# Attention two sequences ahead, 1/sqrt spread through DRAM, one rotation of four PSUM pairs

## The chip, the cores and the metric

The kernel runs on one core of a Trainium2 chip. Its engines are PE (TensorE, matrix products), DVE (VectorE), ACT (ScalarE), POOL (GpSimd) and SP (SyncE, which here issues nearly all DMAs); each runs its own list of instructions in order and waits for others on semaphores. SBUF and PSUM are the on-chip memories of 128 partitions, DRAM the memory outside. The metric is the time of one execution on the device in microseconds. S + x stands for x us after PE begins a sequence.

## The reference

Eight sequences ("batch") of 576 positions go through three stages: linear attention with a norm over each head's 64 features, a gated product with a causal convolution, and a mixing stage.

```python
# attention: q, k, v are (8, 8 heads, 576, 64)
kv = np.einsum('bhsd,bhse->bhde', k, v)
out = np.einsum('bhsd,bhde->bhse', q, kv)
rms = np.sqrt(np.mean(out * out, axis=-1, keepdims=True) + 1e-06)
x = (out / rms * g_norm)            # heads side by side: (8, 576, 512)
# gated product
for k in range(5):
    gate_pre += conv_w[k][None, None, :] * xp[:, k:k + S, :]   # xp: 4 zero rows ahead
gate = 1.0 / (1.0 + np.exp(-gate_pre))
x = gate * (x @ w_val) @ w_out
# mixing
theta = x @ w_theta
yr = np.einsum('ts,bsd->btd', w_tok_r, x * np.cos(theta))
yi = np.einsum('ts,bsd->btd', w_tok_i, x * np.sin(theta))
u = x + yr + yi
out = u + np.maximum(u @ w_ch, 0.0)
```

## The kernel before, in words

Feature d of x lies on a partition, with positions along the free axis, so a 512 x 576 activation is four tiles of 128 x 576. A large product runs in three passes, high x high, high x low, low x high (`product`, L259 to L266); `parts` (L65) makes the high part on ACT (L68) and the low part, the rest, on DVE (L69). Attention and the small selecting products are plain float32, and each of their instructions leaves two records in the trace.

The first phase is the loop over eight sequences at L385. For sequence b these steps exist:
- `key_value` (L171): k transposed times v, 64 x 64 for each head, in PSUM tile kvp, copied by ACT to kvs (L187). It may do all four head pairs, or two of them ("units" of pairs; the table UNITS says how many in which sequence, LEAD how many sequences are done whole at the start).
- `attention` (L189): o = q times kvs in four groups, each two feature tiles by half of the positions (L202); ACT squares each into sq (L206) and copies it, scaled by g_norm, to x (L207). Then `sums` (L214) adds the squares of each head by products with an indicator, into ss: 32 rows for each of the four feature tiles, of which eight are used (two heads by NB = 4 blocks of TB = 144 positions). Twelve DVE operations (L221 to L227) make y, the inverse square root.
- `normalize` (L230): products with the selecting matrix sel (L243) spread y's rows over the 64 partitions of each head into PSUM yb; DVE multiplies x by it in place (L246), and `parts` makes xh and xl. There is one xh and one xl.
- `conv` (L251): the five taps, one on ACT (L253), four on DVE (L255, in acc), then a sigmoid on ACT (L256).
- `value` (L268): four results v of 24 products each (two PSUM banks, 576 positions); DVE multiplies each by the gate in acc (L278), and `parts` makes gh and gl.
- `first` (L284): four results y of 24 products each with w_out. y0 and y1 first use 18 of theirs, and the last six follow when the fourth gh and gl are there. ACT copies y to yo, and SP writes it to DRAM (ydram, L295).

In sequence i the loop does value(i) with the four groups of attention(i + 1) between its results, key/value products of later sequences, then first(i) with the four spreads and multiplies of normalize(i + 1) between its parts. Sequence 0 is prepared ahead of the loop, with key_value(1). Decoding of later weights (w_th and w_tok) goes in at low priority in sequences 1 to 6.

PSUM holds three pairs of banks (pool pd, for v, o, yb and y) and two single banks (pool pk, for kvp and ss). Inputs come by SP in program order: q (`load_q`, buffers q), k and v (`load_kv`, four buffers kv). START is the order of the first loads. No table orders the instructions; a scheduler puts them on each engine when the kernel is built, by priorities and its own costs, and each engine then runs its list as it stands.

The second phase, from L448, computes theta, cosine and sine, token and channel products from what the first left in DRAM.

## Time and profile before

| | us |
|---|---|
| three runs | 779.54, 775.77, 779.06 (median 779.06) |
| the profiled execution | 778.61 |
| its span | 776.7 |
| PE busy in it | 734.6 (95%) |
| DVE busy in it | 532.1 (69%) |
| ACT busy in it | 338.3 (44%) |
| start of theta, the second phase | 342.06 |
| DMA, mean over the span | 126 GB/s |

The page shows the busy time of each engine and groups of instructions by line. A group's row gives the output and inputs by name, the shape, the count, busy time and mean ns of one, and then the idle time of the engine just ahead of them with what ended it. A row of a timeline gives start, length, engine, line, and in brackets the idle time before it and its releaser. A row of windows gives each engine's busy time in a stretch of the span, the granted clock of PE as a share, the DMA engines' share and GB/s. Windows here begin where PE starts a sequence's value product; sequence 0's is at 41.93.

### The profile page before, as it was taken

What the parts mean: (1) busy time and instruction counts of PE and PEld (TensorE: products, weight loads), DVE (VectorE), ACT (ScalarE), POOL (GpSimd) and SP (SyncE); (2) the same over time, 40 slices, a digit from 0 to 9 for tenths busy, and PEclk for the clock granted to TensorE, in tenths of its full rate; (3) what the DMA queues carried; (4) which work ended last, traced back from release to release, by engine and by line L of the source; (5) the groups of instructions that cost most, each with busy time, mean ns of one, the idle gap of its engine ahead of it and who ended that gap; (6) DMA issues with size and microseconds to landing.
All of it is one profiled execution on the core that took longest, in us unless ns stands there. A gap on an engine that the chain in (4) does not pass through costs nothing.

```text
span 776.7 us, 14376 instructions
## 1 busy us (share of the span) xinstructions
PE 734.6 (95%) x5872; PEld 680.0 (88%) x5872; DVE 532.1 (69%) x942; ACT 338.3 (44%) x562; POOL 18.3 (2%) x64
## 2 busy tenths in 40 slices
PE   1588999999999999899999999999999999999998
PEld 1376888888888889898999999899899999999998
DVE  4289778989989796958796493663863853845604
ACT  2246545465636463548462261441651612713301
POOL 3000000000000000000000000000000000000000
PEclk9889999999999999999999999999999999999999
DMA  9956862757373211943606315045033071151101
GB/s 249 261 144 185 261 186 86 192 202 230 131 239 104 62 47 47 271 157 107 185 24 170 101 54 145 35 132 153 2 122 109 31 187 55 45 149 38 62 1 62
DMA packets 72929, 97.56 MB, mean 126 GB/s; under 512 B 10656, under 2 KB 41504, under 8 KB 72864
## 3 DMA queue, kind: packets, MB, share of 16 engines
q1 hardware_dynamic: 72288, 94.55, 40.8%
q0 software_dynamic: 576, 2.10, 0.8%
q8 instruction: 46, 0.75, 0.4%
q14 instruction: 19, 0.16, 0.1%
HBM read 65.66 MB, written 30.97 MB: 124 GB/s over the span
## 4 chain that ended last, share of the span: by engine, by line
PE 77%; DVE 14%; DMA 4%; ACT 3%; issue 2%; SPq 0%; ACTq 0%; DVEq 0%
PE u L508 10%; PE u L506 10%; PE u L507 10%; DVE acc L255 4%; PE c L266 4%; PE c L265 4%; PE c L264 4%; PE y L264 3%; PE th L454 3%; PE th L452 3%; PE th L453 3%; DMA kv<-in_kvm_dram 3%; PE y L266 3%; PE y L265 3%; PE v L264 3%; PE v L265 2%
## 5 line engine op out<-in xcount | busy, mean ns | idle before, releaser
L511 DVE TENSOR_TENSOR f<-u,f 128x288 f32<-128x288 f32 x64 | 26.5, 454 | 128.1 <-PE u L508 128.0
L255 DVE SCALAR_TENSOR_TENSOR acc<-x,cw,acc 128x576 f32<-128x576 f32 x128 | 97.7, 812 | 0.0
L68 ACT ACTIVATE uh<-f 128x288 fp32r<-128x288 f32 x64 | 26.2, 444 | 151.1 <-DVE f L511 151.1
L264 PE MATMUL y<-gh,woh 128*128 128x288 f32 x256 | 79.9, 312 | 3.6 <-DVE acc L278 2.9
L264 PE MATMUL v<-xh,wvh 128*128 128x288 f32 x256 | 79.0, 309 | 3.3 <-ACT wvh L68 3.0
L265 PE MATMUL y<-gh,wol 128*128 128x288 f32 x256 | 77.0, 301 | 0.0
L266 PE MATMUL y<-gl,woh 128*128 128x288 f32 x256 | 76.8, 301 | 0.0
L265 PE MATMUL v<-xh,wvl 128*128 128x288 f32 x256 | 76.1, 298 | 0.3 <-DVE wvl L69 0.3
L266 PE MATMUL v<-xl,wvh 128*128 128x288 f32 x256 | 75.8, 297 | 0.0
L264 PE MATMUL c<-uh,wch 128*128 128x288 f32 x256 | 75.4, 295 | 0.0
L266 PE MATMUL c<-ul,wch 128*128 128x288 f32 x256 | 75.4, 295 | 0.0
L265 PE MATMUL c<-uh,wcl 128*128 128x288 f32 x256 | 75.4, 294 | 0.0
L264 PEld LDWEIGHTS v<-xh,wvh 128*128 128x128 f32 x256 | 48.8, 191 | 14.5 <-issue 8.3
L264 PEld LDWEIGHTS y<-gh,woh 128*128 128x128 f32 x256 | 49.3, 193 | 7.6 <-DVE acc L278 3.4
L454 PE MATMUL th<-wth,yl 128*128 128x512 f32 x128 | 50.3, 393 | 0.0
L453 PE MATMUL th<-wtl,yh 128*128 128x512 f32 x128 | 50.0, 391 | 0.0
L452 PE MATMUL th<-wth,yh 128*128 128x512 f32 x128 | 50.0, 391 | 0.0
L265 PEld LDWEIGHTS y<-gh,wol 128*128 128x128 f32 x256 | 49.5, 194 | 0.5 <-DVE wol L69 0.2
L266 PEld LDWEIGHTS y<-gl,woh 128*128 128x128 f32 x256 | 49.1, 192 | 0.6
L265 PEld LDWEIGHTS v<-xh,wvl 128*128 128x128 f32 x256 | 49.0, 191 | 0.5 <-DVE wvl L69 0.5
L266 PEld LDWEIGHTS v<-xl,wvh 128*128 128x128 f32 x256 | 48.6, 190 | 0.1
L265 PEld LDWEIGHTS c<-uh,wcl 128*128 128x128 f32 x256 | 48.0, 188 | 0.3
(187 smaller groups left out, 1979.9 us busy)
## 6 DMA issues: line engine op xcount, KB each, us to landing
kv<-in_kvm_dram SPq DMA_DIRECT2D x32, 512.0 KB, 6.2
q<-in_qt_dram SPq DMA_DIRECT2D x32, 288.0 KB, 4.5
yd<-yo SPq DMA_DIRECT2D x32, 288.0 KB, 2.2
f<-yd SPq DMA_DIRECT2D x32, 288.0 KB, 3.6
out_dram<-f SPq DMA_DIRECT2D x64, 144.0 KB, 1.8
sd<-fT SPq DMA_DIRECT2D x64, 128.0 KB, 2.5
yt<-sd SPq DMA_DIRECT2D x8, 1024.0 KB, 5.4
raw_tk<-in_w_tok_dram SPq DMA_DIRECT2D x10, 512.0 KB, 5.3
```

The costliest lines, as they stand in the source:

```text
L68: one = nc.scalar.activation(h, src, AF.Copy)
L255: nc.vector.scalar_tensor_tensor(a, x[:, m, k:k + S], cw[:, m * 5 + k:m * 5 + k + 1], a, ALU.mult, ALU.add)
L264: nc.tensor.matmul(ps, wh[:, m, ks], xh[:, k, tsl], start=(k == 0), stop=False)
L265: nc.tensor.matmul(ps, wl[:, m, ks], xh[:, k, tsl], start=False, stop=False)
L266: nc.tensor.matmul(ps, wh[:, m, ks], xl[:, k, tsl], start=False, stop=(k == 3))
L452: nc.tensor.matmul(ps, yh[:, k, :], wth[0][:, k, :], start=(k == 0), stop=False)
L453: nc.tensor.matmul(ps, yh[:, k, :], wth[1][:, k, :], start=False, stop=False)
L454: nc.tensor.matmul(ps, yl[:, k, :], wth[0][:, k, :], start=False, stop=(k == 3))
L506: nc.tensor.matmul(ps[:, :HS], zh[:, ms], wkh[:, j, sl], start=(i == 0), stop=False)
L507: nc.tensor.matmul(ps[:, :HS], zh[:, ms], wkl[:, j, sl], start=False, stop=False)
L508: nc.tensor.matmul(ps[:, :HS], zl[:, ms], wkh[:, j, sl], start=False, stop=(i == 8))
L511: nc.vector.tensor_tensor(f[:, m, sl], ps[:, :HS], f[:, m, sl], ALU.add)
```

## The change

- TB goes from 144 to 72, so y has 64 used rows of 72 instead of 32 of 144: eight blocks of sums, each half as wide.
- key_value does a whole sequence at a time, between the first and the second value result of the sequence two before it; UNITS, LEAD and NBD go.
- attention(i + 2) runs in sequence i: one half (both groups) ahead of the fourth value result, the other half after it; its sums and y follow in first(i), after the second part's last products.
- From sequence 2 on (SPREAD), y is written to DRAM (rdram, new L228) and read back spread over the partitions by two DMAs of 64 partitions (new L233) into yb in SBUF, of which there is one; DVE multiplies from there, two operations of 1152 elements (new L246). Sequences 0 and 1 keep the products with sel (new L254, L257).
- normalize(i + 1) stands between value(i) and first(i).
- One pool of four PSUM pairs serves all; kvp and ss take a pair each and use one bank of it.
- kvs has two buffers instead of four, q two instead of three. START brings k and v of sequence 1 and its q earlier, and three chunks of w_out later. attention(1) and its sums stand ahead of the loop.

```diff
-TB = 144
+TB = 72
 NB = S // TB
...
-NBD = 4
-
-START = "v0 k0 k1 v1 k2 k3 v2 q0 q1 q2 q3 c0 v3 o0 o1 k4 k5 k6 k7 o2 q4 q5 o3 q6 q7"
+
+START = "v0 k0 k1 v1 k2 k3 v2 q0 q1 q2 q3 c0 v3 o0 k4 k5 k6 k7 o1 q4 q5 q6 q7 o2 o3"
 WVFIRST = 3
-WOFIRST = 2
-LEAD = 3
-UNITS = (0, 2, 4, 2, 4, 4, 0, 0, 0)
+SPREAD = 2
...
+    def one_bank(name):
+        return pd.tile([P, 2, 512], F32, tag="pd", name=name)[:, 0, :]
...
+    rdram = [dr.tile([P, TB], F32, tag=f"rd{b}", name=f"rd{b}") for b in range(B)]
...
-    pd = pd_stack.enter_context(tc.tile_pool(name="pd", bufs=3, space=PS))
-    pk = pd_stack.enter_context(tc.tile_pool(name="pk", bufs=2, space=PS))
+    pd = pd_stack.enter_context(tc.tile_pool(name="pd", bufs=4, space=PS))
...
-                q.append(px.tile([P, 2, S], F32, tag="q", bufs=3, name=f"q{b}_{g}"))
+                q.append(px.tile([P, 2, S], F32, tag="q", bufs=2, name=f"q{b}_{g}"))
...
-    def key_value(b, kv, p0=0):
-
-        ps = pk.tile([P, 512], F32, tag="pk", name=f"kvp{b}_{p0}")
-        n = len(kv) // 2
-        for g in range(n):
+    def key_value(b, kv):
+
+        ps = one_bank(f"kvp{b}")
+        for g in range(2):
...
-        if b not in kvs_of:
-            kvs_of[b] = pa.tile([P, NP, D], F32, tag="kvs", bufs=NBD, name=f"kvs{b}")
-        nc.scalar.activation(kvs_of[b][:, p0:p0 + 2 * n, :], ps[:, 0:2 * n * D].rearrange("p (a e) -> p a e", e=D), AF.Copy)
+        kvs_of[b] = pa.tile([P, NP, D], F32, tag="kvs", bufs=2, name=f"kvs{b}")
+        nc.scalar.activation(kvs_of[b], ps[:, 0:NP * D].rearrange("p (a e) -> p a e", e=D), AF.Copy)
...
-                yield x
-
-        sums = pk.tile([P, 512], F32, tag="pk", name=f"ss{b}")[:, :TB]
+            yield x
+
+        sums = one_bank(f"ss{b}")[:, :TB]
...
+        if b >= SPREAD:
+
+            nc.sync.dma_start(out=rdram[b], in_=y)
+            yb = px.tile([P, NM, S], F32, tag="yb", bufs=1, name=f"yb{b}")
+            src = rdram[b].rearrange("(k r) x -> k (r x)", k=NM)
+            for i in range(2):
+                rows = src[:, i * S:(i + 1) * S].unsqueeze(0).to_broadcast([D, NM, S])
+                nc.sync.dma_start(out=yb[i * D:(i + 1) * D], in_=rows)
+            y = yb
         yield x, y
...
-            for g in range(2):
-                yb = two_banks(f"yb{b}_{h}_{g}")
-                for t in range(HS // TB):
-                    for j in range(2):
-                        k = 2 * g + j
-                        rows = slice(32 * k, 32 * (k + 1))
-                        nc.tensor.matmul(yb[:, j, t * TB:(t + 1) * TB], sel[rows, h * HS // TB + t, :], y[rows, :],
-                                         start=True, stop=True, tile_position=(32 * k, 0))
-                ch = slice(2 * g, 2 * g + 2)
-                last = nc.vector.tensor_tensor(v[:, ch], yb, v[:, ch], ALU.mult)
-                if g == 1:
-                    parts(xh[:, :, sl], xl[:, :, sl], v)
-                yield (x, xh, xl), last
+            if b >= SPREAD:
+                last = nc.vector.tensor_tensor(v, v, y[:, :, sl], ALU.mult)
+            else:
+                for g in range(2):
+                    yb = two_banks(f"yb{b}_{h}_{g}")
+                    for t in range(HS // TB):
+                        for j in range(2):
+                            k = 2 * g + j
+                            rows = slice(32 * k, 32 * (k + 1))
+                            nc.tensor.matmul(yb[:, j, t * TB:(t + 1) * TB], sel[rows, h * HS // TB + t, :], y[rows, :],
+                                             start=True, stop=True, tile_position=(32 * k, 0))
+                    ch = slice(2 * g, 2 * g + 2)
+                    last = nc.vector.tensor_tensor(v[:, ch], yb, v[:, ch], ALU.mult)
+            parts(xh[:, :, sl], xl[:, :, sl], v)
+            yield (x, xh, xl), last
...
-            between()
+            between(m)
...
-            last, _ = parts(gh[:, m, :], gl[:, m, :], g)
+            parts(gh[:, m, :], gl[:, m, :], g)
...
         part(0, range(3))
         part(1, range(3))
-        between()
         part(0, (3,))
-        between()
         part(1, (3,))
         between()
         part(2, range(4))
-        between()
         part(3, range(4))
...
     *_, xy = attention(0, qs.pop(0))
+    *_, (xs, last) = normalize(0, *xy)
     key_value(1, kvs.pop(1))
-    *_, (xs, last) = normalize(0, *xy)
+    *_, xy = attention(1, qs.pop(1))
     sg = [conv(0, m, xs[0]) for m in range(EARLY)]
     with tc.issue_after(last.ins):
         for n in range(WVFIRST, 4):
             weight_chunk(px, wv, w_val, n, "wv", raw=raw[f"v{n}"])
-    kvs[2] = load_kv(2)
+    kvs[2], qs[2] = load_kv(2), load_q(2)
     todo = [(wth, w_th, k, "wt", 1.0 / TWO_PI) for k in range(4)]
     toks = list(range(11))
-    units = [(b, p) for b in range(LEAD + 1, B) for p in range(NP)]
     for i in range(B):
         if i == B - 1:
             px_stack.close()
...
             tls = load_tails(0)
             for k in range(CHFIRST):
                 weight_chunk(qx, wch, w_ch, k, "wc")
-        if i + 2 < B:
-            qs[i + 2] = load_q(i + 2)
+        two = i + 2 < B
+        if two:
+            ahead = attention(i + 2, qs.pop(i + 2))
+
+        def between(m):
+
+            if two and m == 1:
+                key_value(i + 2, kvs.pop(i + 2))
+                if i + 3 < B:
+                    kvs[i + 3] = load_kv(i + 3)
+            if two and m == 3:
+                next(ahead)
+
+        gs = value(i, *xs, sg, between)
+        if two:
+            next(ahead)
+            if i + 3 < B:
+                qs[i + 3] = load_q(i + 3)
+        if i + 1 < B:
+            *_, (nxs, last) = normalize(i + 1, *xy)
         if i == 0:
-            for j in range(3, LEAD + 1):
-                kvs[j] = load_kv(j)
-        ahead = units[sum(UNITS[:i]):sum(UNITS[:i + 1])]
-        for b, p in units[sum(UNITS[:i + 1]):sum(UNITS[:i + 2])]:
-            kvs[b, p] = load_kv(b, (p,))[0]
-        nxt = attention(i + 1, qs.pop(i + 1)) if i + 1 < B else iter(())
-        gs = value(i, *xs, sg, (lambda: None) if i == 0 else lambda: next(nxt, None))
-        if i == 0:
-            for k in range(WOFIRST):
+            for k in range(4):
                 weight_chunk(px, wo, w_out, k, "wo", raw=raw[f"o{k}"])
-        xy = (list(nxt) or [None])[-1]
-        if i == 0:
-            for j in range(2, LEAD + 1):
-                key_value(j, kvs.pop(j))
-        for b in range(LEAD + 1, B):
-            ps = [p for c, p in ahead if c == b]
-            if ps:
-                key_value(b, [kvs.pop((b, p)) for p in ps], ps[0])
-        if i == 0:
-            with tc.issue_after(gs[2].ins):
-                for k in range(WOFIRST, 4):
-                    weight_chunk(px, wo, w_out, k, "wo", raw=raw[f"o{k}"])
-        norm = normalize(i + 1, *xy) if i + 1 < B else iter(())
         got = []
-        first(i, *gs[:2], lambda: got.append(next(norm, None)))
+        first(i, *gs, lambda: got.append(next(ahead) if two else None))
+        xy = got[-1]
         if i + 1 < B:
-            xs, last = got[-1]
+            xs = nxs
             sg = [conv(i + 1, m, xs[0]) for m in range(EARLY)]
         if 1 <= i < B - 1:
             with tc.high_priority(offset=-LATER), tc.issue_after(last.ins):```

How it moves instructions, at three places. First PE in sequence 3, in the second stage, behind y3_1's first products (yb is the spread, ss the sums, y the results of the output product, woh and wol the parts of w_out). Before:

```order
L266 MATMUL y3_1_2084<-gl3_1849,woh_129 128x288
L243 MATMUL yb4_0_0_2105<-y4_2028,sel_113 128x144 x4
L243 MATMUL yb4_0_1_2120<-y4_2028,sel_113 128x144 x4
L243 MATMUL yb4_1_0_2137<-y4_2028,sel_113 128x144 x4
L264 MATMUL y3_2_2143<-gh3_1848,woh_129 128x288
```

After:

```order
L276 MATMUL y3_1_2221<-gl3_1968,woh_142 128x288
L212 MATMUL ss5_2258<-sq5_0_0_2133,ind_108 32x72 x2
L212 MATMUL ss5_2258<-sq5_0_1_2141,ind_108 32x72 x2
L212 MATMUL ss5_2258<-sq5_1_0_2177,ind_108 32x72 x2
L212 MATMUL ss5_2258<-sq5_1_1_2185,ind_108 32x72 x2
L274 MATMUL y3_2_2311<-gh3_1967,woh_142 128x288
```

The spread of sequence 4 is gone from PE there, and the sums of sequence 5 stand in its place (each of the four rows comes four times).

Second SP, the queue of DMA issues, at the end of sequence 2 (kv6_0 to kv6_3 are the key and value tiles of sequence 6, yb4 the spread of sequence 4). After the change:

```order
L305 DMA yd2_72<-yo2_3_1913 128x576
L228 DMA rd4_82<-y4_1841 128x72
L156 DMA kv6_0_2047<-in_kvm_dram 128x2x512
L233 DMA yb4_1857<-rd4_82 64x4x576 x2
L157 DMA kv6_0_2047<-in_kvt_dram 64x2x128
L156 DMA kv6_1_2051<-in_kvm_dram 128x2x512
```

The two loads of the spread stand behind the first tile of k and v of sequence 6, and that tile's buffer comes free when key_value(5) has read it in sequence 3.

Third ACT at the start, where conv(0) and attention(1) meet (sq1 are the squares of sequence 1, acc0 the gates of sequence 0). Before:

```order
L256 ACTIVATE acc0_0_409<-acc0_0_409 128x576
L256 ACTIVATE acc0_1_416<-acc0_1_416 128x576
L68 ACTIVATE gh0_477<-acc0_0_409 128x576
L97 ACTIVATE raw_wv_3_163<-raw_wv_3_163 128x512
L68 ACTIVATE wvh_127<-dst_wv_3_423 128x512
L68 ACTIVATE gh0_477<-acc0_1_416 128x576
L256 ACTIVATE acc0_2_507<-acc0_2_507 128x576
L206 ACTIVATE sq1_0_0_628<-o1_0_0_623 128x576
```

After:

```order
L204 ACTIVATE sq1_0_0_461<-o1_0_0_456 128x576
L205 ACTIVATE x1_454<-o1_0_0_456,gsb_60 128x2x288
L266 ACTIVATE acc0_0_537<-acc0_0_537 128x576
L266 ACTIVATE acc0_1_544<-acc0_1_544 128x576
L204 ACTIVATE sq1_0_1_469<-o1_0_1_464 128x576
L205 ACTIVATE x1_454<-o1_0_1_464,gsb_60 128x2x288
L204 ACTIVATE sq1_1_0_477<-o1_1_0_472 128x576
```

The squares of sequence 1 move from behind the third sigmoid to ahead of the first and, three of the four, right behind the second.

More of the change, by code (lines that the diff above doesn't have):

```diff
@@ L278, in value @@
             nc.vector.tensor_tensor(halves(g), ps, halves(g), ALU.mult)
-            last, _ = parts(gh[:, m, :], gl[:, m, :], g)
+            parts(gh[:, m, :], gl[:, m, :], g)
             if m + EARLY < NM:
                 sg.append(conv(b, m + EARLY, x))
-        return gh, gl, last
+        return gh, gl
     def first(b, gh, gl, between):
```

## The prediction

> **What bounds the kernel now.** I read the page first, then windows cut at the starts of the eight sequences, then what PE waited for, then PE's timeline there.
>
> ```profile
> span 776.7 us, 14376 instructions
> PE 734.6 (95%) x5872; PEld 680.0 (88%) x5872; DVE 532.1 (69%) x942; ACT 338.3 (44%) x562; POOL 18.3 (2%) x64
> core 0: us, PE busy (x) PEld busy (x) DVE busy (x) ACT busy (x) POOL busy (x), PEclk, DMA share, GB/s
> 0.00:42.00 42.00, 17.50 (x219) 12.39 (x219) 15.85 (x36) 11.99 (x19) 7.29 (x32) 0.91 0.95 253
> 42.00:63.00 21.00, 17.72 (x134) 16.82 (x134) 19.49 (x27) 8.83 (x13) 0.56 (x2) 0.85 0.51 150
> 63.00:93.60 30.60, 27.66 (x353) 22.42 (x353) 25.23 (x49) 17.98 (x29) 2.42 (x9) 1.00 0.69 213
> 93.60:128.50 34.90, 34.90 (x329) 30.87 (x328) 26.88 (x44) 17.53 (x28) 0.74 (x3) 1.00 0.56 173
> 128.50:165.90 37.40, 36.42 (x369) 32.11 (x368) 34.51 (x60) 21.20 (x34) 1.74 (x5) 1.00 0.66 199
> 165.90:201.20 35.30, 33.82 (x330) 30.25 (x330) 33.62 (x60) 21.04 (x33) 1.18 (x3) 1.00 0.59 190
> 201.20:242.30 41.10, 39.22 (x373) 34.62 (x372) 36.30 (x62) 21.34 (x33) 1.53 (x5) 0.92 0.57 175
> 242.30:278.40 36.10, 36.10 (x373) 32.03 (x372) 29.89 (x55) 19.31 (x31) 0.58 (x1) 1.00 0.18 58
> 278.40:311.90 33.50, 33.50 (x289) 29.66 (x289) 26.15 (x43) 17.27 (x27) 0.00 (x0) 1.00 0.12 42
> 311.90:342.00 30.10, 27.18 (x194) 26.84 (x193) 23.08 (x34) 12.97 (x21) 1.22 (x2) 0.94 0.71 221
> ```
>
> PE sets the time. Sequences 1 to 6 take 218.3 us and PE is busy for 214.0 of them; only the start (to 93.6) and the last sequence leave it idle. The second phase (theta, from 342.06 on) has the same instructions in the same order afterwards, so its 434.6 us stay. The profiled execution took 778.61 us, 1.9 more than its span, and the median of the runs is 779.06, 0.45 more again. What PE waited for in the first phase:
>
> ```profile
> PE yb L243 <- DVE y L227: 7.1, 4, 3.6
> 35.43 1.35 PE L243 MATMUL yb<-y,sel 32*128 32x144 f32 x14 [3.61 <-DVE y L227]
> 41.93 0.61 PE L264 MATMUL v<-xh,wvh 128*128 128x288 f32 x1 [0.35 <-ACT xh L68]
> 57.56 0.40 PE L264 MATMUL v<-xh,wvh 128*128 128x288 f32 x1 [2.95 <-ACT wvh L68]
> 192.14 1.25 PE L243 MATMUL yb<-y,sel 32*128 32x144 f32 x24 [1.12 <-DVE y L227]
> 227.89 0.76 PE L243 MATMUL yb<-y,sel 32*128 32x144 f32 x8 [1.88 <-DVE y L227]
> 328.66 0.61 PE L264 MATMUL y<-gh,woh 128*128 128x288 f32 x1 [2.92 <-DVE acc L278]
> 342.06 0.40 PE L452 MATMUL tht<-wth,th 128*128 128x512 f32 x1
> ```
>
> So there are only 3.0 us of yb waits after the start. Most of what can be won is PE's own work.
>
> **The change part by part, on PE.** The cleanest row is sequence 6 (33.50, all busy): it holds value and output products, one sequence's o, its sums and its spread, and nothing else.
>
> ```profile
> 109.65 1.19 PE L214 MATMUL ss<-sq,ind 128*32 128x144 f32 x32
> 110.77 1.39 PE L183 MATMUL kvp<-kv 128*64 128x64 f32 x40
> 117.05 0.76 PE L243 MATMUL yb<-y,sel 32*128 32x144 f32 x8
> 117.74 0.40 PE L264 MATMUL y<-gh,woh 128*128 128x288 f32 x1
> 218.36 2.55 PE L183 MATMUL kvp<-kv 128*64 128x64 f32 x80
> 278.37 0.72 PE L202 MATMUL o<-q,kvs 64*64 64x288 f32 x8
> 279.01 0.40 PE L264 MATMUL v<-xh,wvh 128*128 128x288 f32 x1
> 25.75 1.21 PE L202 MATMUL o<-q,kvs 64*64 64x288 f32 x16
> ```
>
> Starting from that row, a sequence 1 to 5 of the changed kernel has:
> - no spread on PE. A group of eight records takes 117.74 - 117.05 = 0.69; four groups are 2.76.
> - a whole key/value product, where sequence 6 has none: 80 records, 2.55 with the tail of the last, say +2.45.
> - sums of half the width and twice the number: 64 records of 72 columns for 32 of 144 (110.77 - 109.65 = 1.12). Not shown by this trace. Lower bound 1.12 (the time goes by columns), upper 2.24 (each record costs what it costs now). The nearest row is kvp, 64 columns wide: (2.55 - 1.39)/40 = 29 ns a record, so 64 x 29 = 1.86, and I take +0.74.
> - o in two pairs instead of four single groups: four times 0.64 (279.01 - 278.37) against two times 1.21, and two switches to 288-column products fewer: -0.3.
>
> That makes 33.50 - 2.76 + 2.45 + 0.74 - 0.3 = 33.6, five times 168. [...]
>
> Sequence 6 keeps 33.50 - 2.76 - 2.6 (o) - 1.12 = 27.0 of products; with one more for a late subtraction of parts, 28. Sequence 7 has the same work as before; nothing removes its wait at 328.66, so I leave 30. For waits in sequences 1 to 5 I put 2 us: before, all six had 4.3, of which the yb waits, 3.0, are gone.
>
> **The start.** Key/value product and attention of sequence 1 now stand ahead of value(0), and the sums of sequence 1 too.
>
> ```profile
> 51.94 1.42 ACT L256 ACTIVATE acc<-acc 128x576 f32<-128x576 f32 x2 [3.75 <-DVE acc L255]
> L255 DVE SCALAR_TENSOR_TENSOR acc<-x,cw,acc 128x576 f32<-128x576 f32 x128 | 97.7, 812 | 0.0
> L206 ACT ACTIVATE sq<-o 128x576 f32<-128x576 f32 x32 | 20.6, 644 | 9.4 <-PE o L202 9.4
> ```
>
> On ACT the square sq1_0_1 now stands behind both sigmoids of conv(0), which wait for eight DVE multiply-adds of 0.81 us and end at 51.94 + 1.42 = 53.4. The square takes 0.64, half the sums 0.9 (half of 1.86), so value(0) starts near 55 instead of 41.93. After that PE has v and y 27.0, kvp(2) 2.5, o(2) 2.4, the sums of 2 1.9, half of those of 1 0.9, and yb(1) 2.8: 37.5 us. That alone ends at 92.5. Before, 51.7 us from 41.93 held 38.4 of such work, so 13.3 were waits and a clock granted at 0.85. Most of that, the 2.95 on wvh first, falls away when the decoding has 13 us more; I keep 2.5, which gives 95. Bounds: 88, if value(0) starts at 48 because conv(0) doesn't hold the squares up after all, to 103 (10.5 of the 13.3 stay).
>
> **Sum:** 95 + 168 + 2 + 28 + 30 = 323 for the start of theta, against 342.06: 19.1 less. 778.61 - 19.1 = 759.5; with the 0.45 to the median, 760.
>
> **What hides the spread.** It now runs through DRAM: sums, DVE chain, write, and two loads of 576 KB into 64 partitions each.
>
> ```profile
> q<-in_qt_dram SPq DMA_DIRECT2D x32, 288.0 KB, 4.5
> yd<-yo SPq DMA_DIRECT2D x32, 288.0 KB, 2.2
> yt<-sd SPq DMA_DIRECT2D x8, 1024.0 KB, 5.4
> tok<-td SPq DMA_DIRECT2D x9, 288.0 KB, 2.8
> L69 DVE TENSOR_TENSOR xl<-x,xh 128x1152 fp32r<-128x1152 f32 x16 | 21.7, 1355 | 3.8 <-ACT xh L68 3.8
> L68 ACT ACTIVATE xh<-x 128x1152 fp32r<-128x1152 f32 x16 | 18.6, 1166 | 25.9 <-DVE x L246 25.9
> L246 DVE TENSOR_TENSOR x<-yb,x 128x576 f32<-128x576 f32 x32 | 23.8, 755 | 25.9 <-PE yb L243 25.9
> ```
>
> Issue: in SP's order the spread stands behind kv_0 of three sequences on, whose buffer key_value frees about 4.8 us into the sequence (S + 4.8: v_0 3.4 and half of kvp). Y's chain, twelve short DVE operations between conv's, ends at S + 2 to S + 6 by my count of what stands ahead of it, and its write takes about as long as yo's, 2.2. So the loads start at S + 5.3 to S + 8; at S + 8 the bytes of kv_0 ahead of them are through. Queued behind a late spread are the other kv pieces, q and yo's stores; kv is read a whole sequence later.
>
> Landing: no trace row has a load of this shape. By 128-partition loads, (5.4 - 2.8)/736 KB is 3.5 us a MB: kv_0's 512 KB ahead 1.8, the spread's 1152 KB 4.1, fixed 1.8 (2.8 less 1.0 for its 288 KB): S + 13. By q's 64 partitions, 288 KB take 4.5, 2.7 over the fixed part, so four times 2.7: S + 5.3 + 1.8 + 1.8 + 10.8 = S + 19.7. The two halves go to different partitions and may run side by side, as q's pairs also do, so I take the middle, S + 16.
>
> Deadline: value(i) ends on PE at S + 17.1 (13.5 + 2.45 + 1.2), the last o pair at 18.4, and y_0 and y_1 leave out the last chunk until S + 23.2. From the start of the multiply (DVE L246, now two of 1152 columns, 1.36 each like xl) to gl_3: 2.7, acc_3 0.75, xl 1.36 twice with the wait for xh, gl_3 0.75, some 6.9 in all. So PE stalls when the spread lands after S + 16.3, us for us. At S + 16 it costs nothing. The hiding work is value(i); without it each sequence would pay the 10.7 us from issue to landing. [...]
>
> DVE holds 26 to 27 us of sequence work, and 8 more of weight decoding in three sequences (26.15 against 34.51 and 33.62); the pitch of 33.6 leaves no slack there, and the shorter y rows (72 columns; 305 ns for 144 now) and 4 x 0.755 against 2 x 1.36 give back about 0.8. The spread's 1.18 MB adds 35 GB/s to the 173 to 199 of sequences 1 to 4; the first window shows 253.
>
> **The rivals.**
> - B, the spread lands late, S + 19.7 by q's rate: 3.4 us in each of five sequences, 17 us: 776.5. For it: kv, q and yo share the queues. Against: the halves can overlap.
> - C, the start stays long (103) and DVE adds 0.7 in each of five: 11.5 us: 771.5. For it: DVE busy 44.7 of the 51.6 us up to 93.6.
> - D, slower: the loads crawl like four q loads in a row, 18 us, and land at S + 25: 8.8 us in each of five, 44 us: 803. The gain is gone when the landing passes S + 20.1 (19.1/5 = 3.8 late), slower by 0.5% beyond S + 20.9. For it: q's longest landing:
>
> ```profile
> DMA to landing us min/median/max: 3.7/4.5/11.1
> ```
>
> Against: issued from 94 us on, q lands in 5.5 at most; the long ones are in the first window, where the queues are full (DMA share 0.95).
> - E, it doesn't do what it says: kvp, sums and o fill the space of the spread, and what PE saves is waited elsewhere: 779. Against: sequence 6's row is all PE work.
>
> **How the numbers follow.** Forecast 0.56, with a range of its own of 751 to 770 (start 88 to 103, sums, waits 0 to 5); B 0.17, C 0.14, D 0.09, E 0.04. About 0.5% (3.9 us) is what a measurement of this kernel can tell from no change. Faster by more: 0.56 + 0.14 + half of B 0.09 = 0.79; within: the rest of B and E, 0.11; slower: D, 0.10. The range takes the forecast, C and B: 750 to 777.
>
> **What would show it.** Right: no yb products on PE but those of sequences 0 and 1; a pitch of 33 to 34.5 us in sequences 1 to 5; sums of about 1.9 us; value(0) starting near 55; theta at 320 to 326; a DVE multiply whose releaser is v_2's work, not the spread's load. Wrong: the group DVE x L246 idle for the DMA of yb, and behind it PE waiting for gl or acc in the output stage (B, D); PE waits on acc in value's stage (C); a granted clock below 1.00 in the sequences after such waits.

## The result, and the profile after

The changed kernel takes 753.82 us (median of four runs, 752.95 to 756.92), 0.9693 of the time before (by the means of the runs; 95% interval 0.9655 to 0.9731). 760 was forecast, 750 to 777 as the range. The profiled execution's span went from 776.7 to 751.5 us.

The page of the changed kernel, and windows cut where PE starts each sequence's value product (the last one is the second phase):

```profile
span 751.5 us, 14674 instructions
PE 709.7 (94%) x6000; PEld 669.9 (89%) x6000; DVE 523.9 (70%) x930; ACT 335.9 (45%) x560; POOL 20.7 (3%) x72
core 0: us, PE busy (x) PEld busy (x) DVE busy (x) ACT busy (x) POOL busy (x), PEclk, DMA share, GB/s
0.00:48.50 48.50, 22.51 (x384) 18.68 (x384) 28.52 (x51) 20.37 (x33) 10.90 (x42) 0.88 0.94 258
48.50:89.60 41.10, 40.99 (x467) 36.67 (x466) 38.17 (x74) 24.75 (x40) 1.51 (x5) 0.94 0.74 199
89.60:121.70 32.10, 32.10 (x370) 30.05 (x370) 25.96 (x44) 18.18 (x28) 1.18 (x5) 1.00 0.73 187
121.70:155.90 34.20, 32.68 (x370) 30.09 (x370) 29.58 (x50) 19.48 (x30) 1.19 (x5) 1.00 0.85 220
155.90:189.10 33.20, 32.42 (x371) 29.97 (x370) 29.98 (x51) 19.44 (x31) 1.80 (x5) 1.00 0.85 224
189.10:224.20 35.10, 32.39 (x370) 30.04 (x370) 27.70 (x49) 17.96 (x29) 1.45 (x5) 1.00 0.89 222
224.20:258.90 34.70, 32.69 (x370) 29.95 (x369) 34.35 (x61) 21.37 (x34) 0.39 (x1) 1.00 0.52 159
258.90:286.10 27.20, 25.96 (x194) 25.49 (x193) 25.66 (x44) 14.18 (x23) 0.00 (x0) 1.00 0.51 146
286.10:315.30 29.20, 27.28 (x195) 27.05 (x194) 22.48 (x33) 10.75 (x17) 1.22 (x2) 0.94 0.68 211
315.30:751.50 436.20, 430.65 (x2929) 411.90 (x2928) 261.50 (x484) 169.42 (x301) 1.06 (x2) 1.00 0.31 91
```

PE is busy for 24.9 us less, almost the whole gain of 25.2. Sequence 1 has no wait at all: 32.1 us, all busy. The next four have the same work and PE is idle for 0.8 to 2.7 us in each. Measured by the first value product of each sequence, against before:

| stage | before | forecast | after |
|---|---|---|---|
| start, to sequence 1 | 94.3 | 95 | 89.6 |
| sequences 1 to 5 | 184.8 | 170 | 169.3 |
| sequence 6 | 32.9 | 28 | 27.2 |
| sequence 7 | 30.1 | 30 | 29.2 |
| start of theta | 342.1 | 323 | 315.3 |
| second phase | 434.6 | 434.6 | 436.2 |

The 4.7 us at the start are not all the change's. The first loads of k and v land at other times in each execution: PE's first product of o(0), the attention of sequence 0, starts at 22.25 here and at 23.37 before, and at 19.8 to 25.5 in the profiles further below. From that product to sequence 1 it is 67.3 us, 70.9 before.

What PE waits for in the changed kernel (wkh is the high part of the token weights, which the second phase loads after they were decoded in the first), and DVE's multiply of the spread with the landing of its loads:

```profile
PE y L274 <- DVE acc L288: 5.4, 3, 2.5
PE ss L212 <- ACT sq L204: 4.7, 3, 3.3
PE u L511 <- ACT wkh L68: 2.4, 2, 1.3
PE y L274 <- ACT x L205: 1.4, 4, 0.5
L246 DVE TENSOR_TENSOR x<-x,yb 128x1152 f32<-128x1152 f32 x12 | 15.7, 1354 | 6.2 <-DMA yb<-rd 6.2
DMA to landing us min/median/max: 5.7/8.0/11.2
```

The waits of the spread for y are gone but for the one in the start. In their place DVE waits 6.2 us in three sequences for the spread's loads, and PE waits behind it for v_3's gate multiply (acc): 1.0 us in sequence 2 and 2.5 in sequence 4. The third of the three waits in the first row, 1.9 us, is in sequence 7, where there is no spread. Here are DVE and then PE in sequence 4 (S = 189.06):

```profile
209.07 2.63 DVE L246 TENSOR_TENSOR x<-x,yb 128x1152 f32<-128x1152 f32 x2 [3.40 <-DMA yb<-rd]
211.62 0.75 DVE L288 TENSOR_TENSOR acc<-v,acc 128x576 f32<-128x576 f32 x1
212.43 0.40 PE L274 MATMUL y<-gh,woh 128*128 128x288 f32 x1 [2.51 <-DVE acc L288]
```

The spread lands at S + 20.0, its multiply runs first, and PE's y_1 needs the PSUM pair that the multiply behind it frees.

### The profile page after: what moved, and what is told of

Same layout as the page of the kernel before. It is cut to its first block, busy times and chain, and to the rows that moved or that the text cites. A ratio compares the mean times of both kernels' runs of the same rounds, so it can differ in the third digit from the quotient of the medians.

```text
span 751.5 us, 14674 instructions
## 1 busy us (share of the span) xinstructions
PE 709.7 (94%) x6000; PEld 669.9 (89%) x6000; DVE 523.9 (70%) x930; ACT 335.9 (45%) x560; POOL 20.7 (3%) x72
## 3 DMA queue, kind: packets, MB, share of 16 engines
q1 hardware_dynamic: 76416, 101.85, 48.5%
## 4 chain that ended last, share of the span: by engine, by line
PE 60%; DVE 24%; DMA 8%; ACT 4%; issue 3%; SPq 1%; POOL 0%; DVEq 0%; ACTq 0%; POOLq 0%
PE u L513 10%; PE u L511 10%; PE u L512 10%; DVE acc L265 10%; PE c L276 5%; PE c L274 5%; PE c L275 5%; DMA yb<-rd 4%; PE th L459 3%; PE th L457 3%; PE th L458 3%; DMA kv<-in_kvm_dram 2%; DVE x L246 2%; DVE xl L69 2%; DVE acc L288 2%
## 5 line engine op out<-in xcount | busy, mean ns | idle before, releaser
L265 DVE SCALAR_TENSOR_TENSOR acc<-x,cw,acc 128x576 f32<-128x576 f32 x128 | 100.8, 817 | 1.3 <-ACT acc L263 1.3
L68 ACT ACTIVATE uh<-f 128x288 fp32r<-128x288 f32 x64 | 26.2, 444 | 152.4 <-DVE f L516 152.3
L274 PE MATMUL y<-gh,woh 128*128 128x288 f32 x256 | 77.8, 304 | 7.8 <-DVE acc L288 5.4
L274 PE MATMUL v<-xh,wvh 128*128 128x288 f32 x256 | 77.6, 303 | 0.7 <-DVE acc L288 0.7
L276 PE MATMUL v<-xl,wvh 128*128 128x288 f32 x256 | 76.5, 299 | 0.0
L276 PE MATMUL y<-gl,woh 128*128 128x288 f32 x256 | 75.8, 298 | 0.5 <-DVE gl L69 0.5
L274 PE MATMUL c<-uh,wch 128*128 128x288 f32 x256 | 75.4, 295 | 0.0
L276 PE MATMUL c<-ul,wch 128*128 128x288 f32 x256 | 75.4, 295 | 0.0
L274 PEld LDWEIGHTS y<-gh,woh 128*128 128x128 f32 x256 | 48.8, 191 | 11.9 <-DVE acc L288 6.1
L274 PEld LDWEIGHTS v<-xh,wvh 128*128 128x128 f32 x256 | 48.7, 190 | 4.6 <-issue 1.7
L276 PEld LDWEIGHTS y<-gl,woh 128*128 128x128 f32 x256 | 48.4, 190 | 1.2 <-DVE gl L69 1.2
L276 PEld LDWEIGHTS v<-xl,wvh 128*128 128x128 f32 x256 | 48.6, 190 | 0.3 <-issue 0.2
```

The costliest lines, as they stand in the source:

```text
L68: one = nc.scalar.activation(h, src, AF.Copy)
L265: nc.vector.scalar_tensor_tensor(a, x[:, m, k:k + S], cw[:, m * 5 + k:m * 5 + k + 1], a, ALU.mult, ALU.add)
L274: nc.tensor.matmul(ps, wh[:, m, ks], xh[:, k, tsl], start=(k == 0), stop=False)
L276: nc.tensor.matmul(ps, wh[:, m, ks], xl[:, k, tsl], start=False, stop=(k == 3))
```

## The experiments

Ratios are against the kernel before, measured together with each kernel, so kernels are compared by ratio and not by microseconds. The changed kernel's is 0.9693.

### The spread stays on PE

```diff
-SPREAD = 2
+SPREAD = B
```

> The changed kernel (753.8) with SPREAD = 8: all eight sequences spread 1/sqrt by products with sel on PE, nothing through DRAM; all else as changed. Theory 1 (the gain is PE work that left PE): a spread of 64 records of 72 columns takes 3.77 us on PE in the changed kernel's start (71.69 to 75.46), six sequences get it back, 22.6 us; the waits behind late landings (1.3 and 2.5) go, so about 773. Rival (the gain is the new order, attention in two places, one PSUM rotation, and the DRAM way only replaces something that PE had room for): 753 to 758.

Measured: 0.9889 (0.9856 to 0.9921), 771.35 us. Theory 1 holds against its rival; by ratio the loss is 15 us, less than the 19 expected. The rows are sequence 2 of this kernel, then the stretch of the spread's products in sequence 1 and the 3.4 us after it:

```profile
132.20:170.00 37.80, 37.51 (x435) 35.03 (x434) 33.14 (x59) 21.43 (x32) 1.51 (x5) 0.95 0.64 203
112.50:116.60 4.10, 3.93 (x69) 3.51 (x65) 2.95 (x5) 4.10 (x7) 0.00 (x0) 1.00 0.74 187
116.60:120.00 3.40, 3.40 (x17) 3.40 (x18) 3.40 (x5) 2.64 (x4) 0.00 (x0) 0.62 0.57 126
112.56 4.02 PE L254 MATMUL yb<-y,sel 32*128 32x72 f32 x64
```

Without the DRAM way each of the sequences 1 to 5 takes 37.6 to 37.8 us instead of 32.1 to 35.1. Of the 5.5 us above 32.1 about 4.0 is the spread itself, and the rest goes with the clock, which is granted at 0.62 just behind it. In all the five take 188.1, before 184.8. Sequences 6 and 7 take 54.5 for 63.1; 3.7 of the difference is attention(7), which now stands in sequence 5.

This is the price of the narrow spread, though, and not of the one that the kernel before had. The spread's products keep PE busy for 30.4 us in eight sequences here (512 records of 72 columns) and for 24.4 in the kernel before (256 records of 144), where the clock was 1.00 in five of the sequences 1 to 6. The prediction's row has 2.76 us a sequence for it. A kernel with the rest of the change, TB = 144 and the spread on PE was not run; 32.1 + 2.8 = 34.9 us a sequence is an estimate from these rows. So the run shows that the spread's way off PE is what pays in this kernel, and not how much the rest of the change pays beside a wide spread.

### One sequence ahead

Attention(i + 1) in its two places in sequence i, with sums and y right behind value(i), and normalize(i + 1) behind first(i).

```diff
-            ahead = attention(i + 2, qs.pop(i + 2))
+            ahead = attention(i + 1, qs.pop(i + 1))
...
+            xy = next(ahead)
...
-        if i + 1 < B:
-            *_, (nxs, last) = normalize(i + 1, *xy)
...
-        first(i, *gs, lambda: got.append(next(ahead) if two else None))
-        xy = got[-1]
+        first(i, *gs, lambda: None)
+        if i + 1 < B:
+            *_, (nxs, last) = normalize(i + 1, *xy)
```

> The changed kernel with attention one sequence ahead: attention(i + 1) in its two places in sequence i, its sums and y right after value(i), the DRAM spread as changed, normalize(i + 1) behind first(i). Theory 1 with the lead as what hides it: sums end near S + 20, y and its write near S + 26, loads 8 us: S + 34, multiply and parts 4 more: value(i + 1) starts at S + 38 to 42 instead of S + 32: 6 to 10 us in six sequences, 36 to 60 in all: 790 to 814. Rival (the lead doesn't matter, first(i) is cover enough): under 762.

Measured: 1.0485 (1.0448 to 1.0522), 817.99 us, a little above the range; the mechanism is the one forecast:

```profile
PE v L274 <- ACT xh L68: 40.4, 7, 7.3
```

PE waits 5.3 to 7.3 us at the start of six sequences for xh (1.2 in the seventh). So the lead of two sequences is what hides the DRAM way: with one it costs more than all it saves.

### The loads of k and v behind the spread

```diff
-                    kvs[i + 3] = load_kv(i + 3)
+                    if i + 1 in spread:
+                        with tc.issue_after(spread[i + 1].ins):
+                            kvs[i + 3] = load_kv(i + 3)
+                    else:
+                        kvs[i + 3] = load_kv(i + 3)
```

(spread holds the second load of each sequence's spread.)

> The changed kernel with SP's loads of k and v of sequence i + 3 queued behind the two loads of the spread of i + 1 instead of around them. Theory 2 (what is left of the spread's cost is its place in the queue): the spread lands 2 to 3 us earlier in sequences 2 and 4 (S + 18.5 and S + 20.0 now), the waits of PE behind it (1.3 and 2.5) go, 750 to 751. Rival (it is late because y is late, or the loads are slow by themselves): landing less than 1 us earlier, 753 to 755. Second rival (the keys come late in their turn): waits of kvp on kv after the start, 755 or more.

Measured: 0.9689 (0.9656 to 0.9722), no difference from the changed kernel. The multiply of the spread starts at S + 17.8 in sequence 2 (18.5 without the edit), S + 18.5 in sequence 4 (20.0) and S + 20.3 in sequence 5 (18.6): there one more weight chunk's load goes out just ahead of the spread's on SP, and these take 8.5 to 11.6 us to land instead of 5.7 to 7.7. In sequences 2 and 4 the gain is 0.8 and 1.5 us, not 2 to 3. The loads are not late because of kv_0 alone; theory 2 in this form is refuted.

### Attention(1) back inside sequence 0

```diff
-    *_, xy = attention(1, qs.pop(1))
+    late, hold = attention(1, qs.pop(1)), []
...
+            if i == 0 and m == 1:
+                hold.append(list(late)[-1])
...
+        if i == 0:
+            xy = hold[-1]
```

> The changed kernel with attention(1) and its sums moved from ahead of the loop into sequence 0, between its first and second value result. Theory 3 (the shorter start comes from the work that DVE has no longer to wait for, not from where attention(1) stands): value(0) starts some 4 us earlier than 48.5, sequence 1 starts at 89.6 give or take 2, 752 to 756. Rival (attention ahead of the loop fills a hole of PE that reopens): sequence 1 starts at 93 or later, 757 to 760.

Measured: 0.9709 (0.9680 to 0.9740), an interval that overlaps the changed kernel's. The trace speaks for the rival: value(0) starts at 42.46, but sequence 1 only at 94.65, with PE busy 46.0 of the 52.1 us between, where the changed kernel has 41.0 of 41.1. The first k and v loads landed at about the same time in both (PE starts o(0) at 22.6 and 22.3), so the two starts can be compared. My theory 3 fell: attention ahead of the loop does fill a hole.

### Y's chain ahead of conv on DVE

```diff
+        if m > 0 and b > 0 and b + 1 in ylast:
+            with tc.issue_after(ylast[b + 1].ins):
+                return taps(b, m, x)
...
```

(taps is the old body of conv; ylast holds the last operation of each chain of y.)

> The changed kernel with conv's results 1 to 3 of sequence i + 1 on DVE queued behind the chain that makes y of i + 2. In the changed kernel that chain (twelve operations, 2.8 us) is stretched over 9 us, 84.9 to 93.9 in sequence 0, because each of its steps has a conv operation of 0.81 us ahead of it, and y is written at S + 4.4 to S + 7.1. Theory 2b (the spread is late because y is late): the write moves to before S, the loads start before kv_0 and land at S + 10 or earlier, the multiply no longer waits for them (6.2 us in three sequences now), and of PE's 7 us of waits in sequences 2 to 5 at least 4 go: 0.965 of before or less, against 0.9693. Rival (PE's waits are DVE's order of conv and multiply, whatever the landing): 0.968 to 0.972; second rival (conv is late now, value's gates wait): slower than 0.972.

Measured: 0.9594 (0.9555 to 0.9633), 748.77 us. The number is as theory 2b had it, the reason is not. The loads start at S - 0.9 to S + 3.7 instead of S + 5.9 to S + 8.6, and DVE waits 2.5 us for them instead of 6.2. But sequences 2 to 5 take 33.0 to 34.9 us, 8.9 us in all above 32.1 each, just what they had. PE's waits for the gate multiply in the output stage did fall, from 3.5 to 0.5 us in these four; its waits for ACT's copies of o rose from 2.5 to 5.1. The gain is in sequences 6 and 7 and the second phase. In this kernel, windows of sequences 5, 6, 7 and the second phase:

```profile
227.40:262.00 34.60, 32.45 (x370) 29.93 (x370) 31.32 (x55) 18.43 (x29) 0.12 (x1) 1.00 0.34 93
262.00:287.70 25.70, 25.65 (x194) 25.42 (x193) 25.38 (x33) 15.86 (x24) 0.00 (x0) 1.00 0.65 196
287.70:313.10 25.40, 25.40 (x194) 25.40 (x193) 17.85 (x28) 7.76 (x12) 1.22 (x2) 1.00 0.68 205
313.10:747.00 433.90, 430.31 (x2930) 412.01 (x2928) 260.00 (x482) 168.75 (x300) 1.05 (x2) 1.00 0.31 89
```

51.1 for 56.4 us, and 433.9 for 436.2: in this order the last step of the weight decoding goes out at 249 us instead of 275, PE has hardly a wait in sequences 6 and 7, and waits 0.5 us for wkh. Theory 2b fell as an account of the time; what the spread's lateness costs was still open.

### The PSUM rotation alone

The kernel before, with kvp and sums in one pool of four pairs:

```diff
-    pd = pd_stack.enter_context(tc.tile_pool(name="pd", bufs=3, space=PS))
-    pk = pd_stack.enter_context(tc.tile_pool(name="pk", bufs=2, space=PS))
+    pd = pd_stack.enter_context(tc.tile_pool(name="pd", bufs=4, space=PS))
...
-        ps = pk.tile([P, 512], F32, tag="pk", name=f"kvp{b}_{p0}")
+        ps = one_bank(f"kvp{b}_{p0}")
...
-        sums = pk.tile([P, 512], F32, tag="pk", name=f"ss{b}")[:, :TB]
+        sums = one_bank(f"ss{b}")[:, :TB]
```

(one_bank is that of the changed kernel.)

> The kernel before with only its PSUM changed: one rotation of four pairs for o, v, y, yb, kvp and sums, instead of three pairs and two single banks. Theory 3b (the rotation is what shortens the start): o(0) runs in one piece, as in the changed kernel (22.3 to 24.9, then the sums), y(0) and with it normalize(0) come 3 us earlier, sequence 1 starts 2 to 4 us earlier, and the whole is 0.4 to 0.6% shorter; in the loop it changes nothing. Rival: the rotation makes kvp and sums wait for a pair that DVE or ACT has yet to read, and the loop loses more than the start wins: 1.00 to 1.02.

Measured: 1.0059 (1.0031 to 1.0087). The rival holds. O(0) does run in one piece, and value(0) starts at 39.0 instead of 41.9, but only because k and v landed sooner in this execution: from o(0)'s first product (19.84) to value(0) it is 19.2 us, before 18.6 (from 23.37). And later in the start key/value products wait for a pair:

```profile
73.58 0.44 PE L185 MATMUL kvp<-kv 128*64 128x64 f32 x2 [5.81 <-DVE t L228]
```

Sequence 1 starts at 96.2 (94.3 before). By itself the rotation is a small loss.

### Sums of full width

```diff
-TB = 72
+TB = 144
```

> The changed kernel with TB = 144: sums of 32 records of 144 columns, y of 32 used rows, the spread through DRAM as changed. Theory (records of the sums cost by columns: 64 of 72 took 1.13 us, 32 of 144 took 1.12): PE unchanged; DVE has twelve y operations of 0.30 for 0.23, 0.9 us more a sequence, and y is later by the same: 0.969 to 0.974. Rival (the half width is a part of the gain): over 0.975.

Measured: 0.9726 (0.9681 to 0.9771), inside the range, but for reasons that partly cancel, none of them the one given. The start is 4 us shorter (sequence 1 at 85.9), sequences 6 and 7 are 3.9 shorter, sequences 1 to 5 take 169.9 for 169.3, and PE then waits 13.1 us in the second phase for the token weights, where the changed kernel waits 2.4:

```profile
PE u L511 <- ACT wkh L68: 13.1, 1, 13.1
```

### One more copy on the spread's way

```diff
+    hdram = [dr.tile([P, TB], F32, tag=f"hd{b}", name=f"hd{b}") for b in range(B)]
...
-            nc.sync.dma_start(out=rdram[b], in_=y)
+            nc.sync.dma_start(out=hdram[b], in_=y)
+            nc.sync.dma_start(out=rdram[b], in_=hdram[b])
```

> The changed kernel with one more copy of y, 37 KB from DRAM to DRAM, between its write and the spread's loads: the landing moves by the time of one small transfer, about 2 us. Theory 2 (late landings stall PE us for us where there is no slack): the sequences 2 and 4, which wait already (1.3 and 2.5), lose 2 each, 1, 3 and 5 lose what exceeds 1 to 2 of slack: 4 to 8 us in all, 0.974 to 0.980. Rival (slack is large, waits have another cause): under 0.972.

Measured: 0.9753 (0.9706 to 0.9800), inside theory 2's range, and again not for its reason. The spread's multiply starts at S + 19.4, 21.4, 21.3, 22.6 and 19.9, later than in the changed kernel by 1 to 4 us, and PE's waits for v_3's gate multiply in the output stage nearly vanish (0.28 in one place). Sequences 1 to 5 are 1.5 us shorter in all and 6 and 7 are 4.3 shorter. Against that the second phase is 12.0 us longer, with a wait of 12.2 us for wkh, and the start is 1.5 longer. SP in this kernel, and then the same loads in the changed one (td is the last decoded piece of the token weights on its way to DRAM, f what the second phase loads of the first's results):

```profile
297.85 0.32 SPq L442 DMA_DIRECT2D td<-dst_tk  x1
298.26 0.86 SPq L332 DMA_DIRECT2D f<-yd  x2
```

```profile
275.49 0.85 SPq L330 DMA_DIRECT2D f<-yd  x2
282.49 1.62 SPq L330 DMA_DIRECT2D f<-yd  x1
```

The last step of decoding stands behind conv(7) on DVE here (at 297.6), its DMA goes out at 297.9, and the loads for the second phase come behind it on SP, 16 to 23 us later than in the changed kernel. In DVE's order of this build v_3's multiply stands ahead of the spread's in sequences 1 to 4; the additional copy is the only edit, so the scheduler moved it on that account.

### The copy again, decoding in time

```diff
-            with tc.high_priority(offset=-LATER), tc.issue_after(last.ins):
+            with tc.high_priority(offset=-LATER if i < 4 else 0), tc.issue_after(last.ins):
```

> The kernel with the additional DRAM copy (0.9753), and the low priority of the last three weight chunks' decoding taken off (sequences 4 to 6), so that the last step of it stands ahead of conv(7) on DVE again. Theory 4 (the 12 us that the copy seemed to cost were not the late spread but one step of decoding, which DVE had put off to 297.6, and behind whose DMA on SP the loads for the second phase stood, 298.3 instead of 282.5): PE's wait for wkh goes from 12.2 to under 3, and the kernel takes 0.959 to 0.966 of before, faster than the changed one although its spread lands 1 to 4 us later, because v_3's gate multiply now stands ahead of the spread's multiply on DVE. Rival (the late landing does cost, the wait for wkh was only where it showed): 0.970 to 0.976.

Measured: 0.9670 (0.9619 to 0.9722), 752.82 us. The wait for wkh is 2.4 us, as theory 4 said. The time lies between the two expectations: sequences 1 to 5 take 167.8 us in all, as with the copy alone, and 6 and 7 lose 3.0 to the decoding. With the copy, and the orders that came with it, the kernel is as fast as the changed one, although the spread's multiply starts 0.7 to 5.8 us later. Where it starts latest, at S + 23.1 and S + 23.3 in sequences 3 and 4, PE does wait 0.8 and 1.0 us for gl.

### V_3's multiply ahead of the spread's

The changed kernel with DVE's order as the copy had it, and the decoding in time (the edit above):

```diff
-            *_, (nxs, last) = normalize(i + 1, *xy)
+            with tc.issue_after(gs[2].ins) if i > 0 else ExitStack():
+                *_, (nxs, last) = normalize(i + 1, *xy)
...
```

(gs[2] is the gate multiply of v_3.)

> The changed kernel with DVE's multiply of the spread (of i + 1) queued behind the gate multiply of v_3 (of i), and the decoding's low priority taken off in sequences 4 to 6 as above; no additional copy. Theory 4b (what the spread still costs in the changed kernel is v_3's multiply queued behind it on DVE): PE's waits for DVE's gate multiply in the output stage (5.4 us in three places) go, first phase 5 to 8 us shorter, 0.958 to 0.965. Rival (the waits move to xh and xl, which value(i + 1) needs): waits of v for xh, 0.968 to 0.972.

Measured: 0.9605 (0.9554 to 0.9657), 747.55 us. Windows of sequences 1 to 6:

```profile
90.80:122.90 32.10, 32.10 (x371) 30.05 (x370) 24.69 (x43) 18.03 (x28) 1.18 (x5) 1.00 0.73 193
122.90:155.00 32.10, 32.10 (x370) 30.05 (x370) 30.11 (x52) 19.46 (x30) 1.23 (x5) 1.00 0.85 210
155.00:187.10 32.10, 32.10 (x370) 30.05 (x370) 28.83 (x48) 18.50 (x29) 1.35 (x5) 1.00 0.84 237
187.10:220.40 33.30, 32.39 (x369) 29.87 (x369) 30.48 (x54) 19.10 (x31) 1.36 (x5) 1.00 0.93 251
220.40:252.80 32.40, 32.19 (x370) 30.06 (x369) 31.60 (x56) 21.70 (x35) 0.24 (x1) 1.00 0.56 167
252.80:283.00 30.20, 27.80 (x195) 27.12 (x194) 28.52 (x48) 15.32 (x23) 0.00 (x0) 0.94 0.49 149
```

Three sequences in a row run at 32.1 with no idle time on PE, and sequences 1 to 5 together stand 1.6 us above that instead of 8.9. Sequences 2 and 3 lie ahead of the decoding that the second edit touches (sequences 4 to 6), and that edit alone left sequences 1 to 5 of the kernel with the copy at 167.8 in all. DVE in sequence 4 (S = 187.06):

```profile
204.59 0.75 DVE L288 TENSOR_TENSOR acc<-v,acc 128x576 f32<-128x576 f32 x1
207.13 1.36 DVE L246 TENSOR_TENSOR x<-x,yb 128x1152 f32<-128x1152 f32 x1 [1.79 <-DMA yb<-rd]
```

The spread lands at S + 20.1 here, as late as in sequence 4 of the changed kernel (S + 20.0), and PE's wait of 2.5 us behind it is gone. So this much is settled: a landing that late costs PE no wait by itself; v_3's multiply queued behind the spread's does. PE's waits for ACT's copies of o went from 2.5 to 0.7 us in sequences 2 to 5 too. The edit changed the order on ACT and DVE around them; which part of that did it was not separated. Sequence 6 is 3.0 us longer, with more of the decoding in it, and sequence 7 is 2.9 shorter.

### Full width, decoding in time

> The kernel with TB = 144 (0.9726) and the decoding's low priority taken off in sequences 4 to 6. In the wide kernel PE waited 13.1 us for wkh, and its first phase ended at 308.2, 7 us before the changed kernel's. Theory 4 (that wait is the same put-off step of decoding): the wait goes, 0.955 to 0.962, and so the half width of the sums is no gain but a loss of a few us, at the start (the squares of sequence 1 stand ahead of the sigmoids there). Rival (half width is a gain of its own): over 0.968.

(TB = 144 and the decoding's edit.) Measured: 0.9655 (0.9594 to 0.9716), 750.93 us: the wait for wkh fell from 13.1 to 3.3, but the time is above the expected range, with 2.7 us more in sequences 6 and 7, where the decoding now stands. The interval takes in the changed kernel's 0.9693, so half width is not shown to be a loss or a gain. The start stays short (sequence 1 at 85.7). Here as in the wide kernel PE has no long wait for the squares of sequence 1 (3.3 us in the changed one): in this build ACT has all of them ahead of the two sigmoids. That is the order that the scheduler made for this width.

### Full width, with y's chain ahead

> The two edits that gave most, together: TB = 144 and the chain of y ahead of conv's results 1 to 3 on DVE (0.9594 alone). If their gains add (start 3 to 4 us, no put-off decoding since it ends early here): 0.952 to 0.957, the best version. If they overlap: 0.958 to 0.962.

(TB = 144, and y's chain ahead of conv.) Measured: 0.9530 (0.9480 to 0.9580), 741.68 us, the fastest of all: sequence 1 at 86.2, sequences 6 and 7 in 51.6 us, second phase 434.0. By the middle value the gains add; the interval ends where the expectation for overlapping gains begins. Of single edits, v_3's multiply ahead (0.9605, with the decoding in time) came closer to y's chain than full width did. Putting v_3's multiply first as well was not tried.

## Why the prediction was right, and where its steps were off

**170 us for sequences 1 to 5 against 169.3 is in part luck.** The work was 7.5 us too high (33.6 for 32.1, five times) and the waits 6.9 too low.

**The spread leaves PE: right.** The sum gave 33.6 us a sequence; without waits it is 32.1, and with the narrow spread kept on PE 37.6. Two other terms were mis-sized. The products of value and output were taken as 27.0 from sequence 6 of the kernel before, which has them cut in eight places by o and yb; uninterrupted they take 25.4 (the window 287.70:313.10 above). The narrow sums were taken as 1.86:

```profile
114.06 1.21 PE L212 MATMUL ss<-sq,ind 128*32 128x72 f32 x64
115.20 0.40 PE L274 MATMUL y<-gh,woh 128*128 128x288 f32 x1
```

They take 1.14 (115.20 - 114.06), the lower bound: with 64 records of 72 columns in 1.14 and 32 of 144 in 1.12, the time goes by columns here. 64 records in 1.14 us start 18 ns apart, against the 29 of the kvp row that the 1.86 was worked out from.

**Waits in sequences 1 to 5: 8.9 us instead of 2.** PE is idle for 7.0 of it, and the first product behind a pause takes longer (0.40 us at 212.43, 0.29 or 0.30 those behind it). This is rival B in part: 3.8 of the 7.0 stand behind a late spread (1.3 in sequence 2, 2.5 in sequence 4), 2.5 are waits for ACT's copies of o, which the prediction did not have, and 0.7 is a wait for a gate multiply in the value stage. The spread landed at S + 15.6, 18.5, 16.4, 20.0 and 16.9, against a middle forecast of S + 16 and B's S + 19.7; its multiply started at S + 15.6, 18.5, 17.3, 20.0 and 18.6. The step "PE stalls when the spread lands after S + 16.3, us for us" failed: landings at S + 18.5 and S + 20.0 cost 0.9 and 1.2 less than that, and those at S + 16.4 and S + 16.9 nothing. The limit itself was no property of the chain but of DVE's order, in which acc_3 stands behind the spread; with acc_3 ahead, a landing at S + 20.1 cost nothing. From the first issue to the last landing the middle forecast has 10.7 us, and 8.3 to 11.9 were measured; the loads started at S + 5.8 to 8.6, where the prediction has S + 5.3 to S + 8.

**The start: 89.6 instead of 95.** The step that failed is that conv(0)'s two sigmoids end at 53.4. They end at 46.8:

```profile
45.42 1.41 ACT L266 ACTIVATE acc<-acc 128x576 f32<-128x576 f32 x2 [1.68 <-DVE acc L265]
47.43 1.17 PE L212 MATMUL ss<-sq,ind 128*32 128x72 f32 x28 [3.31 <-ACT sq L204]
48.53 0.61 PE L274 MATMUL v<-xh,wvh 128*128 128x288 f32 x1
```

I had moved a time of the old start into the new one, where sequence 0's spread comes 3.5 us sooner (31.97 for 35.43; 1.1 of that because o(0) starts sooner in this execution) and DVE has the multiply-adds of conv(0) nearly by themselves. The wait of the squares behind them is there as forecast, 3.3 us. So the lower bound's time came true, value(0) at 48, but not its reason, that conv(0) doesn't hold the squares up. From value(0) to sequence 1 I had 40 us, measured 41.0. The 89.6 is a favourable execution: in the six other profiles whose program is the same up to value(0) (the spread on PE, k and v later, y's chain ahead, v_3's multiply ahead, and the copy twice), value(0) starts at 49.6 to 53.1 and sequence 1 at 90.8 to 94.6, so part of the distance from 95 is luck.

**Sequences 6 and 7** came within 0.9 us. What I had not seen is that both hang on where the decoding stands: 56.4 us here, with its last steps in sequence 6 (the last goes out at 275), 51.1 where it is through at 249, and 52.0 with the copy, where the last step is put off to 297.9. The last way is paid for in the second phase.

**The second phase does not stay as it is**: 436.2 for 434.6. It has the same order, but its first products wait 2.4 us for the token weights, 0.6 before; the last step of the decoding goes out at 275 instead of 262. "The same instructions in the same order" was no ground for the same time.

**Rivals C, D and E** did not come. DVE's 34.35 busy of 34.70 in sequence 5 is the one place where C's mechanism, DVE full of decoding, was near. D, a landing at S + 25, was far: no landing passed S + 20.0. (C's 771.5 is counted from 760, B's and D's times from 759.5; and the rest of B and E are 0.125, D alone 0.09, where the prediction has 0.11 and 0.10.)

**The signs.** Of those named for "right", only the products of yb came out as named. The sums take 1.14 for 1.9, value(0) starts at 48.5 for 55, theta at 315.3 for 320 to 326, and sequences 1 to 5 take 32.1 to 35.1 for 33 to 34.5. In three sequences the multiply's releaser is the load, which was a sign for B.

## What to carry to other kernels

Ask whether the engine that a step moves off is busy all the time, and how much lead hides the new way: here, with PE busy for 32.10 of 32.1 us in sequence 1, the way off PE was worth 5.5 us a sequence for the narrow spread with two sequences of lead (2.8 for the spread as it was, an estimate from the row of 2.76), and a loss with one (1.0485). The late transfer hurt here through what stood behind its consumer in DVE's list (2.5 us of PE at S + 20.0, no wait at S + 20.1 with v_3's multiply ahead), so look there for an operation that others wait for, before making the transfer earlier. When an edit changes the scheduler's order, compare all stages: twice a small edit moved the last step of a background job behind the foreground and made another phase 12 to 14 us longer.

## What the runs showed of the hardware that I had not expected

PE's clock fell while PE was busy: in the kernel with the spread on PE, PE was busy for 3.93 of 4.1 us of the spread's products (32 rows of weights, 72 columns), and in the next 3.4 us the granted clock was 0.62. The same fall followed the spread in each of its sequences 0 to 5: an output product takes 0.29 us ahead of it and 0.44 or 0.45 in it. In the changed kernel's start the same 64 records (71.69 to 75.46, PE busy for 3.66 us of 3.77) left the clock at 1.00. Nor is the place what decides: behind these products in the same place of the start, in rows of the same 3.77 or 3.78 us, the output products go from 0.29 to 0.44 or 0.45 us in the kernel with y's chain ahead, the two with the copy and the one with the spread on PE, and stay at 0.29 or 0.30 in those with the loads of k and v later and with v_3's multiply ahead. What tells them apart stays open.

Two loads of 64 partitions each, 1.18 MB together, took 5.7 to 11.2 us each to land beside other traffic. With the spread in the queues the median landing of kv is 8.6 us, 6.6 in the kernel with the spread on PE and 6.2 before. That of q is 8.9, 7.5 with the spread on PE and 4.5 before, so most of q's rise comes with the new order of the loads and not with the spread. After the start PE never waits for either.
